# One weight load ahead of the attention loads, and weight splits held until the first block's last x

## The chip, the cores and the metric

The kernel runs on one core of a Trainium2 chip. The metric is the device time of one execution in microseconds (us); lower is better. TensorE (PE) has two clock levels, 1.2 and 2.4 GHz; the profile gives the granted clock as a share of the full one.

## The reference

The reference is a block-causal attention whose result goes through a mixture of four experts. Cut to what matters:

```python
# q, k, v: (4 batches, 8 heads, 576 positions, 64)
mask = pos_q // 64 >= pos_k // 64
attn = softmax(where(mask, q @ k.T / 8, -1e9)) @ v
x = attn.transpose(0, 2, 1, 3).reshape(2304, 512)
p = domain_probs / (domain_probs.sum(-1) + 1e-9)
for e in range(4):                       # w1[e]: 512 x 1024, w2[e]: 1024 x 512
    out += p[:, e:e+1] * (relu(x @ w1[e]) @ w2[e])
```

All data is fp32. The kernel gets enough precision out of fast matmuls by splitting every operand into a high half (a cast) and a low half (the operand minus the cast) and adding three products: high by high, low by high and high by low.

## The kernel before

**Tiles.** The 2304 tokens are cut into five blocks. Block 0 holds the first 64 positions of all four batches (256 tokens); blocks 1 to 4 hold the other 512 positions of one batch each. The attention of a block gives x, transposed, as `xh` (high) and `xl` (low). Block 0 needs only the first 64 keys, and a routine of its own, `first_block`, computes it in four steps (`step`, each one half of the batches and two of the four 128-row parts of x): transposes (L834), scores (L854), softmax on VectorE (DVE, L869 to L879) and ScalarE (ACT, L873), a transpose back (L883), the product with v (L896), and then the cast `xh` (L345) and the subtraction `xl` (L352). The steps run staggered; while PE has nothing to do in this prologue the program puts filler matmuls in (L364).

**Experts.** A chunk is one expert and 128 of its 1024 hidden columns: 32 chunks per block, numbered through. For each chunk `mm1` (L1013) forms h from x and w1 in 12 matmuls (four parts of x by three products), `relu` makes `hh` (ACT, L1030) and `hl` (DVE, L1032), and `mm2` (L1063) adds h by w2 to the accumulators (6 matmuls for block 0). Chunk i's mm2 is asked for after mm1 of chunk i + 1. Blocks 3 and 4 are done together, two chunks at a time, by seven products in place of eight (`product`, L1236), whose operands S1 to S4 are sums of x parts and whose weights `w1rp`, `w1l` and the like are sums of w1 quarters; `scp` are copies and sums of product results.

**Weights.** Each raw chunk of w1 and w2 is 256 KB. `w_load` brings it from memory into one of three buffers (`w1r`, `w2r`); `w_split` casts the high half (`w1h`, `w2h`, L345, ACT or DVE) and subtracts for the low half (`w1l`, `w2l`, L352, DVE). The raw buffer is free for the chunk three later as soon as both halves are there.

**Attention of the other blocks.** It goes on beside the expert matmuls, a pair of heads (a unit) at a time: K and Q are loaded (`kr`, `qr`), transposed on DVE (`kT` L415, `qT` L449), multiplied on PE (L509 and its kin, 2 groups of matmuls for the first units), and the scores are copied out by ACT (`S`, `cm`, masks L556).

**What sets the order.** No engine chooses at run time. A list scheduler, `Flow`, writes the whole program while the kernel is built: every operation has a cost, a priority (lower goes first) and inputs, the scheduler keeps a modelled clock for each engine, and it emits the operation that can start first, the lower priority number deciding among equals. Each engine then works through its own list in that order and stops at an instruction whose inputs are not there. All loads of raw weights, K, most of Q, and V stand in one list, that of SyncE (SP). While chunk 0 is at work (`now[0] == 0`), `w_prio` (L924) gives raw weights 1.6 (chunk 0) or 2.005 (all others); the next attention's K and Q have 2.00 and its V 2.005. A tuple `("until", condition)` holds a thread of the scheduler until the condition is true. `left_first[0]` counts the steps of `first_block` whose `xl` has not been emitted: 4 at the start, 0 after the last.

Of the kernel before, what the change touches and what calls it, by code (L numbers as in the profile page):

```python
# [210 lines left out]
def kernel(  # L211
# [131 lines left out]
    def a_copy(dst, src, n, r, u, prio=0.0, ps=False):  # L343
        engs = [("act", 0.833 * n + (55 if ps else 95)), ("dve", (1.04 if ps else 0.52) * n + 70)]
        o = op(engs, 0, lambda e: nc.scalar.copy(dst, src) if e == "act" else nc.vector.tensor_copy(dst, src), r, u, prio)  # L345
        o.port = not ps
        return o

    def tt(eng, dst, a, b, alu, n, r, u, prio=0.0):
        both = {"dve": 1.04 * n + 70, "pool": 2.1 * n + 365}  # L350
        engs = [(e, both[e]) for e in (eng if isinstance(eng, list) else [eng])]
        o = op(engs, 0, lambda e: ENG[e].tensor_tensor(out=dst, in0=a, in1=b, op=alu), r, u, prio)  # L352
        o.port = a.space != PSUM and b.space != PSUM
        return o
# [24 lines left out]
    now, loads = [0], [0]  # L379
    left_first = [len(STEPS)]  # L380
# [542 lines left out]

    def w_prio(i, which):  # L924
        i -= 4 * (i >= NC) * (which == 1)
        return lambda: (1.6 if i == 0 else 2.005) if now[0] == 0 else 1.0 if i <= now[0] + 1 else (2.5 if i <= now[0] + 2 else 5.0)

    def w_load(which, i, e, f):
        raw = yield fl.take(f"w{which}r")
        pr = w_prio(i, which)  # L930
        src = w1[e, :, f * P:(f + 1) * P].rearrange("(c p) f -> p c f", p=P) if which == 1 else w2[e, f * P:(f + 1) * P, :]
        v0 = yield dma(raw.tile, src, P * DM * 4, u=[raw], prio=pr)
        return raw, v0, pr

    def w_thread(which):
        for i, (_, e, f) in enumerate(chunks + [(PAIR, e, f) for e in range(E) for f in range(FC)]):
            if which == 1 and i >= NC:
                break
            raw, v0, pr = yield from w_load(which, i, e, f)
            fl.spawn(w_split(which, i, raw, v0, pr))  # L940
        if which == 1:
            for j, (e, f) in enumerate(pairs):
                got = []
                for k in range(2):
                    got.append((yield from w_load(1, NC + 2 * j + k, e, f + k)))
                fl.spawn(w_pair(j, *got))

    def flat(raw):
        return raw.tile.rearrange("p c f -> p (c f)") if len(raw.tile.shape) == 3 else raw.tile

    def halves(which, turn, src, n, deps, raw, pr, more=()):

        hi = yield fl.take(f"w{which}h", turn)
        lo = yield fl.take(f"w{which}l", turn)
        a = yield a_copy(hi.tile[:, :n], src, n, deps, [raw, hi], pr)
        o = tt(BOTH, lo.tile[:, :n], src, hi.tile[:, :n], SUB, n, deps + [a], [raw, hi, lo], pr)
        o.pen = lambda: 1000.0 if now[0] == 0 else 300.0
        l = yield o
        return hi, lo, a, l

    def w_split(which, i, raw, v0, pr):
        wt[i, which] = yield from halves(which, i, flat(raw), DM, [v0], raw, pr)
        fl.give(raw)

# [428 lines left out]
```

## Time and profile before

| what | us |
| --- | --- |
| median of 3 runs (lowest to highest) | 904.07 (903.63 to 905.41) |
| the profiled execution, its own time | 903.51 |
| span of the profiled execution, first to last instruction | 901.6 |
| PE busy in it | 890.2 |
| DVE busy in it | 692.3 |
| ACT busy in it | 451.8 |

The span is what the rows can explain; 1.9 us of the profiled execution lie around it. A row of a timeline gives start, duration, engine, line, operation, output and inputs, and in brackets the idle time of the engine before it and what ended that. The program's names come without buffer numbers there.

### The profile page before, as it was taken

What the parts mean: (1) busy time and instruction counts of PE and PEld (TensorE: products, weight loads), DVE (VectorE), ACT (ScalarE), POOL (GpSimd) and SP (SyncE); (2) the same over time, 40 slices, a digit from 0 to 9 for tenths busy, and PEclk for the clock granted to TensorE, in tenths of its full rate; (3) what the DMA queues carried; (4) which work ended last, traced back from release to release, by engine and by line L of the source; (5) the groups of instructions that cost most, each with busy time, mean ns of one, the idle gap of its engine ahead of it and who ended that gap; (6) DMA issues with size and microseconds to landing.
All of it is one profiled execution on the core that took longest, in us unless ns stands there. A gap on an engine that the chain in (4) does not pass through costs nothing.

```text
span 901.6 us, 12364 instructions
## 1 busy us (share of the span) xinstructions
PE 890.2 (99%) x4302; PEld 715.3 (79%) x4302; DVE 692.3 (77%) x1298; ACT 451.8 (50%) x857; POOL 140.6 (16%) x53
## 2 busy tenths in 40 slices
PE   8999999999999999999999999899999999999998
PEld 4778787787877877877877877688888888888886
DVE  6799999888988987988988888975566655566542
ACT  3587766564646556557645643545343333333220
POOL 1101110322133134124142232000000000000000
PEclk9999999999999999999999999999999999999999
DMA  9775457544535354634435332322120212110002
GB/s 179 171 199 168 146 142 185 157 109 96 144 95 126 103 128 104 172 118 114 103 109 118 93 95 75 123 72 59 35 68 27 82 35 71 48 48 24 12 1 94
DMA packets 214654, 91.17 MB, mean 101 GB/s; under 512 B 130368, under 2 KB 195904, under 8 KB 214592
## 3 DMA queue, kind: packets, MB, share of 16 engines
q1 hardware_dynamic: 211424, 89.59, 37.9%
q10 hardware_dynamic: 3168, 0.79, 0.5%
q8 instruction: 34, 0.56, 0.3%
q14 instruction: 28, 0.23, 0.1%
HBM read 85.63 MB, written 4.72 MB: 100 GB/s over the span
## 4 chain that ended last, share of the span: by engine, by line
PE 93%; DVE 3%; DMA 2%; SPq 1%; issue 0%; ACT 0%; DVEq 0%; ACTq 0%
PE h L1013 24%; PE acc L1063 23%; PE acc L1299 19%; PE h L1236 9%; PE att L1236 7%; PE att L733 4%; PE att L521 2%; PE att L522 2%; PE att L509 1%; PE acc L733 1%; DMA w1r<-in_moe_w_dram 1%; SPq L339 1%; DMA S<-in_v_dram 1%; PE acc L509 1%; DVE xr L352 1%; DMA cm<-in_q_dram 0%
## 5 line engine op out<-in xcount | busy, mean ns | idle before, releaser
L1013 PE MATMUL h<-xl,w1h 128*128 128x512 f32 (+1 forms) x384 | 136.5, 356 | 1.9 <-DVE xl L352 1.9
L1013 PE MATMUL h<-xh,w1h 128*128 128x512 f32 (+1 forms) x384 | 137.5, 358 | 0.0
L1013 PE MATMUL h<-xh,w1l 128*128 128x512 f32 (+1 forms) x384 | 136.5, 355 | 0.0
L1063 PE MATMUL acc<-w2h,hh 128*128 128x512 f32 x316 | 125.1, 396 | 0.0
L1063 PE MATMUL acc<-w2l,hh 128*128 128x512 f32 x316 | 123.4, 391 | 0.0
L1063 PE MATMUL acc<-w2h,hl 128*128 128x512 f32 x316 | 123.2, 390 | 0.0
L345 ACT CAST w2h<-w2r 128x512 fp32r<-128x512 f32 x113 | 70.4, 623 | 68.1 <-PE acc L1063 56.3
L666 POOL PARTITION_ALL_REDUCE sb<-sa x24 | 80.4, 3400 | 136.2 <-DVE sa L352 102.0
L687 POOL PARTITION_ALL_REDUCE mx<-cm x16 | 56.0, 3501 | 274.2 <-DVE cm L352 237.4
L352 DVE TENSOR_TENSOR w1l<-w1r,w1h 128x512 fp32r<-128x512 f32 (+1 forms) x124 | 86.5, 698 | 1.2 <-ACT w1h L345 0.3
L1030 ACT ACTIVATE hh<-h 128x512 fp32r<-128x512 f32 (+1 forms) x95 | 49.9, 526 | 72.0 <-PE h L1013 71.6
L352 DVE TENSOR_TENSOR w2l<-w2r,w2h 128x512 fp32r<-128x512 f32 x117 | 79.5, 680 | 4.7 <-ACT w2h L345 4.4
L1013 PEld LDWEIGHTS h<-xl,w1h 128*128 128x128 f32 x384 | 73.1, 190 | 12.4 <-DVE xl L352 2.1
L1013 PEld LDWEIGHTS h<-xh,w1h 128*128 128x128 f32 x384 | 72.9, 190 | 11.6 <-issue 1.2
L1013 PEld LDWEIGHTS h<-xh,w1l 128*128 128x128 f32 x384 | 73.0, 190 | 10.3
L345 ACT CAST w1h<-w1r 128x512 fp32r<-128x512 f32 (+1 forms) x111 | 66.1, 595 | 15.7 <-DMA w1r<-in_moe_w_dram 8.0
L1063 PEld LDWEIGHTS acc<-w2h,hl 128*128 128x128 f32 x316 | 59.3, 188 | 13.0
L1063 PEld LDWEIGHTS acc<-w2h,hh 128*128 128x128 f32 x316 | 59.5, 188 | 12.7 <-issue 1.7
L345 ACT COPY S<-att 128x512 f32<-128x512 f32 (+2 forms) x95 | 50.9, 536 | 34.6 <-DVE att L591 24.1
L1063 PEld LDWEIGHTS acc<-w2l,hh 128*128 128x128 f32 x316 | 59.5, 188 | 10.3
L1032 DVE SCALAR_TENSOR_TENSOR hl<-h,hh 128x512 fp32r<-128x512 f32 (+1 forms) x95 | 56.0, 589 | 9.9 <-ACT hh L1030 9.2
L352 DVE TENSOR_TENSOR S<-S,mx 128x1024 f32<-128x1024 f32 (+4 forms) x80 | 59.8, 790 | 3.3 <-POOL mx L687 3.1
(331 smaller groups left out, 1819.3 us busy)
## 6 DMA issues: line engine op xcount, KB each, us to landing
w2r<-in_moe_w_dram SPq DMA_DIRECT2D x128, 256.0 KB, 2.9
w1r<-in_moe_w_dram SPq DMA_DIRECT2D x120, 256.0 KB, 2.9
qr<-in_q_dram SPq DMA_DIRECT2D x112, 64.0 KB, 2.3
kr<-in_k_dram SPq DMA_DIRECT2D x64, 72.0 KB, 2.9
VN<-in_v_dram SPq DMA_DIRECT2D x32, 128.0 KB, 2.5
out_dram<-o SPq DMA_DIRECT2D x12, 256.0 KB, 2.1
w1rp<-in_moe_w_dram SPq DMA_DIRECT2D x8, 256.0 KB, 2.8
out_dram<-op SPq DMA_DIRECT2D x4, 256.0 KB, 2.1
```

The source lines that it names most:

```text
L345: o = op(engs, 0, lambda e: nc.scalar.copy(dst, src) if e == "act" else nc.vector.tensor_copy(dst, src), r, u, prio)
L352: o = op(engs, 0, lambda e: ENG[e].tensor_tensor(out=dst, in0=a, in1=b, op=alu), r, u, prio)
L509: nc.tensor.matmul(out=o, lhsT=KK.tile[hp, k0:k0 + n], rhs=qT.tile[hp, lo:W], start=True, stop=True)
L666: sums.append((yield op("pool", 150 + 6.3 * W, lambda _, h=h: nc.gpsimd.partition_all_reduce(sb.tile[:, h * W:h * W + W], sa.tile[:, h * W ...
L687: lambda _: nc.gpsimd.partition_all_reduce(mx.tile[:, :2 * W], src, P, RED.max),
L733: nc.tensor.matmul(out=x.tile[64 * g:64 * g + 64, W - w:W], lhsT=lhsT, rhs=rhs, start=(i == 0), stop=(i == len(todo) - 1))
L1013: nc.tensor.matmul(out=ps[:, :n], lhsT=s.tile[:, ks], rhs=x.tile[:, kc, :n], start=(kc == 0 and m == 0), stop=(kc == KC - 1 and m == 2),)
L1030: a = yield op("act", 0.833 * n + 55, lambda _: nc.scalar.activation(hh.tile[:, :n], ps[:, :n], AF.Relu), [mm], [pb, hh], 0.0)
L1032: l = yield op("dve", 1.04 * n + 70, lambda _: nc.vector.scalar_tensor_tensor(out=hl.tile[:, :n], in0=ps[:, :n], scalar=0.0, in1=hh.tile[: ...
L1063: nc.tensor.matmul(out=acc, lhsT=s.tile[:, ts], rhs=w.tile, start=(f == 0 and m == 0), stop=(f == FC - 1 and m == 2))
L1236: nc.tensor.matmul(out=ps[:, :n], lhsT=w.tile[:, ks], rhs=x[:, kc, :n], start=(start and kc == 0 and m == 0), stop=(i in (2, 3, 4) and kc ...
L1299: nc.tensor.matmul(out=acc, lhsT=s.tile[:, ts], rhs=w.tile, start=(c == 0 and x == 0), stop=(c == 3 and x == 2))
```

## The change

Two edits. In `w_prio`, while chunk 0 is at work, the raw w1 of chunk 1 (i = 1, which = 1) gets priority 1.7, which is ahead of K, Q and V of the next attention. In `w_split`, every split but those of w1 of chunks 0 and 1 waits until all four steps of the first block have their `xl` emitted.

```diff
     def w_prio(i, which):
         i -= 4 * (i >= NC) * (which == 1)
-        return lambda: (1.6 if i == 0 else 2.005) if now[0] == 0 else 1.0 if i <= now[0] + 1 else (2.5 if i <= now[0] + 2 else 5.0)
+        return lambda: (1.6 if i == 0 else 1.7 if i + which == 2 else 2.005) if now[0] == 0 else 1.0 if i <= now[0] + 1 else (2.5 if i <= now[0] + 2 else 5.0)
...
     def w_split(which, i, raw, v0, pr):
+        if i + which > 2 or (i, which) == (0, 2):
+            yield ("until", lambda: left_first[0] == 0)
         wt[i, which] = yield from halves(which, i, flat(raw), DM, [v0], raw, pr)
         fl.give(raw)
```

`i + which == 2` also holds for (0, 2), the w2 of chunk 0, but there the first condition, i == 0, has been taken. Lines behind L961 are two higher in the changed kernel.

Since the scheduler lists everything anew, the order changes on every engine from the prologue on. In DVE's list, at the end of the first block, the last two `xl` stood like this before (`xl_93` is x's low half; chunk n's halves have the numbers 61 + n, 65 + n, 69 + n and 73 + n for w1h, w1l, w2h and w2l):

```order
L352 TENSOR_TENSOR w1l_66<-w1r_78,w1h_62 128x512
L352 TENSOR_TENSOR xl_93<-acc_131,xh_91 128x2x128
L345 CAST w1h_63<-w1r_79 128x512
L352 TENSOR_TENSOR w1l_67<-w1r_79,w1h_63 128x512
L345 CAST w2h_70<-w2r_81 128x512
L352 TENSOR_TENSOR w2l_74<-w2r_81,w2h_70 128x512
L352 TENSOR_TENSOR xl_93<-acc_130,xh_91 128x2x128
L415 STREAM_TRANSPOSE kT_110<-kr_107 128x576
```

and stand like this now:

```order
L878 RECIPROCAL st_98<-st_98 128x4
L879 TENSOR_TENSOR o_90<-o_90,st_98 128x256
L352 TENSOR_TENSOR xl_93<-acc_131,xh_91 128x2x128
L352 TENSOR_TENSOR xl_93<-acc_133,xh_91 128x2x128
L415 STREAM_TRANSPOSE kT_110<-kr_107 128x576
L352 TENSOR_TENSOR w2l_73<-w2r_80,w2h_69 128x512
L352 TENSOR_TENSOR w1l_67<-w1r_79,w1h_63 128x512
L352 TENSOR_TENSOR w2l_74<-w2r_81,w2h_70 128x512
```

The last two `xl` follow one another; w1 of chunk 2 and w2 of chunk 1 (two casts and two subtractions), which stood between them, went to ACT (casts) and behind `xl` (subtractions), and so did w2l of chunk 0. The split of chunk 1's w1 (`w1h_62`, `w1l_66`), which stood ahead of the third `xl`, is now some rows earlier, among the softmax of the third step.

In ACT's list behind the last `xh`, before (`hh_83` is chunk 0's relu and `w2h_72` the cast of chunk 3's w2; `S`, `cm` belong to the first unit):

```order
L345 CAST w2h_71<-w2r_82 128x512
L1030 ACTIVATE hh_83<-h_128 128x256
L345 CAST w1h_64<-w1r_77 128x512
L345 CAST w2h_72<-w2r_80 128x512
L345 COPY S_120<-acc_132 128x512
L345 COPY cm_122<-acc_132 128x64
```

and now, some rows further on, where `hh_83` is chunk 2's relu and `w1h_62` the cast of chunk 5's w1:

```order
L345 COPY cm_122<-att_134 128x64
L556 ACTIVATE att_135<-ident 64x64 x2
L556 ACTIVATE acc_133<-ident 64x64 x2
L345 CAST w2h_72<-w2r_80 128x512
L345 COPY S_120<-att_135 128x512
L345 CAST w1h_62<-w1r_79 128x512
L556 ACTIVATE acc_132<-ident 64x2x64
L1032 ACTIVATE hh_83<-h_128 128x256
```

The cast of chunk 3's w2 left its place ahead of the scores' copies; it stands behind two of them, two `cm` copies and four masks now, four rows ahead of the relu of chunk 2.

In SP's list, where that w2 is loaded (`w2r_80`), before (`kr_108`, `VN_117` and `probs_n` are K, V and the domain probabilities for unit 1 and block 0):

```order
L339 DMA kr_108<-in_k_dram 32x18x32 x2
L339 DMA w2r_80<-in_moe_w_dram 128x512
L339 DMA kr_108<-in_k_dram 32x18x32
L339 DMA VN_117<-in_v_dram 128x64
L339 DMA VN_117<-in_v_dram 128x4x64
L339 DMA VN_117<-in_v_dram 128x64
L339 DMA VN_117<-in_v_dram 128x4x64
L339 DMA probs_n<-in_moe_domain_probs_dram 64x4 x4
```

and now (`w1r_78` is chunk 4's w1, `kr_107` is K of unit 2):

```order
L339 DMA kr_108<-in_k_dram 32x18x32 x3
L339 DMA VN_117<-in_v_dram 128x64
L339 DMA VN_117<-in_v_dram 128x4x64
L339 DMA w1r_78<-in_moe_w_dram 128x4x128
L339 DMA VN_117<-in_v_dram 128x64
L339 DMA VN_117<-in_v_dram 128x4x64
L339 DMA probs_n<-in_moe_domain_probs_dram 64x4 x4
L339 DMA kr_107<-in_k_dram 32x18x32 x4
L339 DMA w2r_80<-in_moe_w_dram 128x512
```

`w2r_80` moved behind V, the probabilities, chunk 4's w1 and the four loads of unit 2's K. Ahead of this place, chunk 1's `w1r_78` moved from behind unit 0's K, Q and V to ahead of them; the three raw loads that followed it (`w1r_79`, `w2r_81`, `w2r_82`) kept their places.

In DVE's list in the stage of the two blocks together (`scp` are sums of products, and `w1l_65` is the low half of the sum `w1rp` of w1 quarters), before:

```order
L352 TENSOR_TENSOR scp_4856<-h_128,scp_4859 128x512
L352 TENSOR_TENSOR w1l_68<-w1rp_4851,w1h_64 128x256
L352 TENSOR_TENSOR w2lp_4850<-w2r_82,w2hp_4848 128x512
L352 TENSOR_TENSOR w1rp_4851<-w1rp_4851,w1r_79 128x256
L1281 SCALAR_TENSOR_TENSOR hlp_4841<-scp_4856,hhp_4837 128x512
L352 TENSOR_TENSOR scp_4858<-scp_4857,scp_4858 128x512
L352 TENSOR_TENSOR w2l_74<-w2r_80,w2h_70 128x512
L352 TENSOR_TENSOR w1l_65<-w1rp_4851,w1h_61 128x512
```

and now, starting two rows behind the same first sum `scp`, which is `scp_4858` here:

```order
L352 TENSOR_TENSOR w2l_74<-w2r_80,w2h_70 128x512
L352 TENSOR_TENSOR w1rp_4853<-w1rp_4853 128x256
L352 TENSOR_TENSOR scp_4860<-scp_4859,scp_4860 128x512
L1283 SCALAR_TENSOR_TENSOR hlp_4843<-scp_4858,hhp_4839 128x512
L352 TENSOR_TENSOR w1l_68<-w1rp_4853,w1h_64 128x256
L352 TENSOR_TENSOR w2l_75<-w2r_81,w2h_71 128x512
L1283 SCALAR_TENSOR_TENSOR hl_86<-scp_4860,hh_84 128x512
L1283 SCALAR_TENSOR_TENSOR hlp_4844<-att_135,hhp_4840 128x512
L352 TENSOR_TENSOR w1rp_4853<-w1rp_4853,w1r_79 128x256
L352 TENSOR_TENSOR w2l_76<-w2r_82,w2h_72 128x512
L352 TENSOR_TENSOR xr_100<-att_134,xr_100 128x512
L352 TENSOR_TENSOR w1l_65<-w1rp_4853,w1h_61 128x512
```

`w1l_65` stands seven rows behind the first `scp` sum before, and thirteen behind it now. In PE's list the last 1525 instructions, from this stage on, are the same in both.

## Rows read from the trace of the kernel before

**Rows 1.** The page's first part: engine, busy time, share of the span, instructions.

```profile
PE 890.2 (99%) x4302; PEld 715.3 (79%) x4302; DVE 692.3 (77%) x1298; ACT 451.8 (50%) x857; POOL 140.6 (16%) x53
```

**Rows 2.** PE's waits: line, what was waited for, total, times, longest.

```profile
PE att L1236 <- ACT scp L1256: 2.0, 2, 1.4
PE h L1013 <- DVE xl L352: 1.9, 1, 1.9
```

**Rows 3.** PE's timeline, from block 0's first mm1 to unit 1's scores.

```profile
24.61 0.28 PE L1013 MATMUL h<-xh,w1h 128*128 128x256 f32 x1
26.76 0.58 PE L1013 MATMUL h<-xl,w1h 128*128 128x256 f32 x1 [1.86 <-DVE xl L352]
...
29.06 0.41 PE L1013 MATMUL h<-xh,w1l 128*128 128x256 f32 x1
29.40 1.03 PE L509 MATMUL acc<-qT,kT 64*128 64x512 f32 x1
...
31.71 0.39 PE L1013 MATMUL h<-xh,w1h 128*128 128x256 f32 x1
...
37.99 0.28 PE L1013 MATMUL h<-xh,w1h 128*128 128x256 f32 x1
...
39.42 0.40 PE L1063 MATMUL acc<-w2h,hh 128*128 128x512 f32 x1
...
43.03 0.69 PE L509 MATMUL att<-qT,kT 64*128 64x512 f32 x1
...
45.01 0.50 PE L1063 MATMUL acc<-w2h,hh 128*128 128x512 f32 x1
```

**Rows 4.** A stretch of core 0: us, busy time by engine, granted clock (PEclk), DMA.

```profile
26.70:30.10 3.40, 3.34 (x13) 2.93 (x15) 3.23 (x7) 1.41 (x3) 0.00 (x0) 0.50 0.72 169
```

**Rows 5.** DVE's timeline around the last `xl` of block 0.

```profile
24.15 0.43 DVE L345 CAST w1h<-w1r 128x512 fp32r<-128x512 f32 x1 [1.02 <-DMA w1r<-in_moe_w_dram]
...
25.68 0.69 DVE L352 TENSOR_TENSOR w2l<-w2r,w2h 128x512 fp32r<-128x512 f32 x1
26.29 0.42 DVE L352 TENSOR_TENSOR xl<-acc,xh 128x256 fp32r<-128x256 f32 x1
26.62 0.77 DVE L415 STREAM_TRANSPOSE kT<-kr 128x576 f32<-128x576 f32 x1
```

**Rows 6.** ACT's timeline: the last `xh`, a weight cast, a relu.

```profile
24.04 0.37 ACT L345 CAST xh<-acc 128x256 fp32r<-128x256 f32 x1 [1.20 <-PE acc L896]
...
37.09 0.61 ACT L345 CAST w2h<-w2r 128x512 fp32r<-128x512 f32 x1
...
39.63 0.38 ACT L1030 ACTIVATE hh<-h 128x256 fp32r<-128x256 f32 x1 [1.44 <-PE h L1013]
```

**Rows 7.** SP's issues; a row can hold several, as xN says.

```profile
24.32 1.02 SPq L339 DMA_DIRECT2D w2r<-in_moe_w_dram  x1
25.39 0.43 SPq L339 DMA_DIRECT2D kr<-in_k_dram  x1
...
28.14 2.43 SPq L339 DMA_DIRECT2D probs_n<-in_moe_domain_probs_dram  x4
30.67 1.08 SPq L339 DMA_DIRECT2D w1r<-in_moe_w_dram  x2
...
33.40 2.84 SPq L339 DMA_DIRECT2D qr<-in_q_dram  x4
```

**Rows 8.** Raw w2 loads issued up to 45 us, from issue to landing.

```profile
DMA to landing us min/median/max: 3.3/4.0/7.0
```

**Rows 9.** PE's timeline in the stage of two blocks together.

```profile
579.08 0.49 PE L1236 MATMUL att<-S4h,w1h 128*128 128x512 f32 x1 [1.37 <-ACT scp L1256]
...
583.76 0.39 PE L1236 MATMUL h<-S2h,w1l 128*128 128x512 f32 x1
```

**Rows 10.** DVE's timeline in the same stage.

```profile
577.21 0.68 DVE L352 TENSOR_TENSOR scp<-h,scp 128x512 f32<-128x512 f32 x1
...
580.88 0.68 DVE L352 TENSOR_TENSOR w1l<-w1rp,w1h 128x512 fp32r<-128x512 f32 x1
```

## The prediction

> **What bounds the kernel now.** I read the page's first part: PE is busy 890.2 of 901.6 us [rows 1], so only a wait or a slow clock on PE can give time back, and only a new PE wait can take it. PE's waits come second [rows 2]: two causes of some size are left, one `h<-xl` wait of 1.9 us in the first block and two `scp` waits of 2.0 us in all in the stage of two blocks together. The timeline of PE [rows 3] shows the first: the matmul at 26.76 had waited 1.86 us for block 0's last `xl`. DVE's timeline [rows 5] says why `xl` was late. ACT had the last `xh` at 24.04 + 0.37 = 24.41 [rows 6], but DVE was at four weight instructions, the first of which waited 1.02 us for its load (24.15), and `xl` ran from 26.29 to 26.71. The windows [rows 4] show the price behind the wait: the granted clock was 0.50 from 26.7 to 30.1, that is 1.2 GHz.
>
> **The last x.** Each term is made against the profiled execution, 903.51 us; the median is 904.07, so I add 0.56 at the end. In DVE's new order the last `xl` follows the third, with no weight work between. Chunk 1's cast and subtraction stand among the softmax now and w2l of chunk 0 has left it, so the softmax carries one cast more, 0.43 us [rows 5]; part of it falls into gaps between dependent steps, and I take 0.3 (bounds 0 to 0.43). `xh` then ends at 24.71, `xl` 0.42 later at 25.13, and with the 0.05 us between `xl` and matmul that 26.71 and 26.76 show, PE goes on at 25.18. That is 1.58 us earlier. PE has hardly a wait left there: its first seven matmuls end at 24.61 + 0.28, and 0.3 later than that.
>
> **The clock.** Without the pause I expect no slow stretch. From 26.76 to 29.40 stand eleven matmuls in 2.64 us [rows 3]; at the full clock twelve of the same kind take 39.42 - 37.99 = 1.43, so eleven take 1.31: 1.33 lost. The first group of scores took 31.71 - 29.40 = 2.31, its twin of unit 1 took 45.01 - 43.03 = 1.98: 0.33 lost. The two edits' gain is 1.58 + 1.33 + 0.33 = 3.24.
>
> **What the held splits cost at once.** The weight work that stood ahead of `xl` stands behind it. ACT does four casts behind the last `xh`, of 0.61 us at most [rows 6], 2.0 to 2.4 in all, then chunk 0's relu of 0.38: 27.1 to 27.5. PE has 5 + 12 matmuls to do meanwhile, 2.02 us, until 27.2. Its third matmul of mm2 needs `hl`, which on DVE stands behind `kT` (0.77 [rows 5]) and three subtractions (0.61 each by the starts 25.68 and 26.29): 25.13 + 0.7 + 1.83 + 0.42 = 28.1, against a need at some 27.7. That is 0.4. The scores need `qT`, one subtraction and one transpose behind `hl`, 29.3 against 29.0: 0.3. Together +0.7 (0 to 1.2, the upper end if both relu and `hl` are at their late ends).
>
> **Chunk 3's w2.** This is the term that I trust least. Before, its load was issued at 24.32 [rows 7]. Now fourteen issues come ahead of it from that place on: one K, four V, four probabilities, one w1, four K. Before, the nine issues from 25.39 to 30.67 took 0.59 each; the four Q from 33.40 on took 0.71 each, and a lone K 0.43. So the load is issued at 24.32 + 14 x 0.59 = 32.6 (30.3 to 34.3), and 4.0 us later (3.3 to 7.0 [rows 8]) it has landed: 36.6. ACT's list has the cast, a score copy, the next cast, masks and then chunk 2's relu, some 2.2 us as the sum of three times 0.61 and 0.38 [rows 6], so `hh` of chunk 2 is there at 38.8. What is queued behind the waiting cast is that relu, and PE waits for it with mm2 of chunk 2. PE was there at 39.42 [rows 3]; with 3.24 gained and 0.7 lost it is there at 36.9. New wait: 38.8 - 36.9 = 1.9. Ends: 30.3 + 3.3 + 2.2 = 35.8, no wait at all, and 34.3 + 7.0 + 2.2 = 43.5, 6.6 us.
>
> The row at 24.15 shows a cast that stood still for its load with `xl` behind it [rows 5]. The Trainium skill says the same for ACT (Perfetto Trace Analysis, Per-engine timelines): ACT, DVE and GpSimd are strict first-in first-out queues. It speaks against this change: by it the relu, whose h is long ready, cannot pass the cast. If it could, this term would be zero and the sum 1.9 lower.
>
> **Later loads.** Behind that w2 two more raw loads are issued, then eight loads of Q and probabilities and only then w1 of chunk 6: 32.6 + 3 x 0.59 + 2.84 + 2.43 = 39.6 [rows 7]. The weights of chunks 6 and 7 and w2 of chunk 5 thus come about 2 us later than before, but PE too is late by now, and they are wanted some chunks further on. I take +0.4 (0 to 2).
>
> **The stage of two blocks.** No operation is added there, yet DVE's list changed. `w1l_65` ended at 580.88 + 0.68 = 581.56 [rows 10], 2.2 us ahead of its use at 583.76 [rows 9]. Now twelve instructions stand between the sum `scp` and it: eight of 512 columns at 0.6 and four of 256 columns at 0.33 (the starts 26.29 and 26.62 in [rows 5]), so that with `scp` itself it starts 0.6 + 4.8 + 1.3 = 6.7 behind `scp`'s start (before: 580.88 - 577.21 = 3.7). Directly ahead of S4's low half three subtractions took the place of one cast and two small sums, 0.5 more. End: 577.21 + 0.5 + 6.7 + 0.68 = 585.1, which is 1.35 us late. The copies that the wait of 1.37 at 579.08 [rows 9] hangs on might come up to 0.3 us sooner, but `w1l_65` is last then, so that gains nothing. +1.35 (0, if DVE gets ahead earlier in the stage, to 1.9).
>
> **The sum.** -3.24 + 0.7 + 1.9 + 0.4 + 1.35 = +1.1: 904.6 for the profiled execution, 905.2 as a median.
>
> **Rivals.**
> First, the gain stays. If SP issues at the pace of the lone K (0.43), chunk 3's w2 is there in time and the loads behind it too: -3.24 + 0.7 + 1.35 = -1.2, a median of 902.9; if DVE also catches up in the late stage, -2.5, 901.5. [...] Against it: the nine issues at 0.59 were the same V and probabilities.
>
> Second, slower: the new wait costs the clock too. A pause of 1.86 us was followed by a stretch at 0.50 [rows 3, 4], while behind the pause of 1.37 matmuls took 0.39 [rows 9], as at full clock. A wait of 1.9 for chunk 3's w2 lies at the upper of these; from about there on, the 1.66 us of clock loss come back, and 905.2 becomes 906.9. With the slowest landing of [rows 8], 3 us above the 4.0, it would be 909 or more.
> [...]
>
> Third, the change does not do what it says. If chunk 1's w1 has not landed when its cast comes up among the softmax, DVE stops there, as it did for 1.02 us at 24.15, and the last `xl` is no earlier by that much: about +1 us, 906.2, or more if the clock falls as before.
>
> **How the numbers follow.** Forecast 905.2 with 0.45; the gain stays 0.27; the clock falls again or the load lands late 0.23; no earlier x 0.05. A run can tell about 0.2%, 1.8 us, from no change, so faster means below 902.3 and slower above 905.9. The first rival lies below 902.3 in about half of its cases, and 0.03 of the forecast with it: 0.17. The forecast's own spread (903.5 to 906.8, from the bounds of the small terms) puts 0.15 of it above 905.9; with 0.21 of the second rival and 0.05 of the third, slower has 0.41. Within 0.2% is left with 0.42: 0.27 of the forecast, 0.13 of the first rival, 0.02 of the second. The range reaches to both neighbours: 901.4, the first rival's lower time, to 908.3, between the two prices of the second.
>
> **What would show it.** In the changed kernel's profile: PE's wait `h<-xl` gone or under 0.4, no stretch at half clock from 25 to 30 us, the first mm2 at about 27.2 with a short wait for `hl`. SP issues `w2r` of chunk 3 past 32 us, and ACT stands before its cast with `<-DMA w2r`. PE waits for ACT's `hh` at about 37 us, 1 to 2 us long. Near 580 us PE waits for `w1l<-w1rp` or its cast. I am wrong if `w2r` is issued before 30.5 us, or if the late stage waits as before, or if a new wait shows between 45 and 560 us, where I put none.

## The result, and the profile after

| kernel | median, us | lowest to highest | ratio to before, 95% interval |
| --- | --- | --- | --- |
| before | 903.85 (6 runs) | 901.54 to 905.69 | |
| changed | 908.58 (6 runs) | 907.80 to 909.54 | 1.0058 [1.0040, 1.0076] |

The change costs 4.7 us. Slower was the forecast's sign, but the time lies 3.4 us above the 905.2 forecast and just outside the range. The profiled execution of the changed kernel took 908.19 us, its span is 906.4.

The page's first part of the changed kernel (engine, busy time, share, instructions) answers to [rows 1]; PE's work is the same, and its share fell:

```profile
PE 890.0 (98%) x4304; PEld 711.7 (79%) x4305; DVE 693.1 (76%) x1300; ACT 449.2 (50%) x855; POOL 142.8 (16%) x53
```

PE's waits in the changed kernel (line, what was waited for, total, times, longest) answer to [rows 2]; rows of the prologue are left out:

```profile
PE acc L1065 <- ACT hh L1032: 2.3, 2, 1.3
...
PE att L1238 <- ACT scp L1258: 1.4, 2, 0.7
PE att L733 <- DVE cm L352: 0.9, 2, 0.5
...
PE acc L509 <- ACT cm L345: 0.8, 1, 0.8
PE h L1238 <- ACT w1h L345: 0.7, 1, 0.7
...
PE h L1238 <- DVE w1l L352: 0.4, 1, 0.4
...
PE att L522 <- DVE LL L352: 0.3, 1, 0.3
PE att L570 <- DVE cm L352: 0.2, 1, 0.2
```

The wait for `xl` is gone. In its place stand two for a relu (`hh`), one for a copy of scores, four small ones for DVE in the middle of the kernel, and two for weights in the late stage. The slow stretch of [rows 4] is gone too. The same window in the changed kernel (us; busy time of PE, PEld, DVE, ACT, POOL; granted clock; DMA share; GB/s) reads:

```profile
26.70:30.10 3.40, 3.39 (x18) 1.95 (x19) 2.61 (x5) 1.73 (x5) 0.00 (x0) 1.00 0.41 90
```

PE's timeline answers to [rows 3]. The idle time in brackets understates a wait, since the matmul behind it also holds up its successor (the start after 36.54 comes 0.34 us later, where 0.23 is usual):

```profile
25.95 0.40 PE L1065 MATMUL acc<-w2h,hh 128*128 128x512 f32 x1
26.18 0.40 PE L1065 MATMUL acc<-w2l,hh 128*128 128x512 f32 x1
26.61 0.50 PE L1065 MATMUL acc<-w2h,hl 128*128 128x512 f32 x1
...
27.83 0.69 PE L509 MATMUL acc<-qT,kT 64*128 64x512 f32 x1
...
36.54 0.50 PE L1065 MATMUL acc<-w2h,hh 128*128 128x512 f32 x1 [0.99 <-ACT hh L1032]
...
43.87 0.50 PE L1065 MATMUL acc<-w2h,hh 128*128 128x512 f32 x1 [1.27 <-ACT hh L1032]
...
51.38 0.43 PE L509 MATMUL acc<-qT,kT 64*128 64x192 f32 x1 [0.76 <-ACT cm L345]
```

ACT's timeline in the same stretch shows what the two relus stood behind:

```profile
34.26 0.62 ACT L345 CAST w2h<-w2r 128x512 fp32r<-128x512 f32 x1 [2.96 <-DMA w2r<-in_moe_w_dram]
34.79 0.58 ACT L345 COPY S<-att 128x512 f32<-128x512 f32 x1
35.26 0.62 ACT L345 CAST w1h<-w1r 128x512 fp32r<-128x512 f32 x1
...
36.12 0.36 ACT L1032 ACTIVATE hh<-h 128x256 fp32r<-128x256 f32 x1
...
41.42 0.62 ACT L345 CAST w1h<-w1r 128x512 fp32r<-128x512 f32 x1 [3.35 <-DMA w1r<-in_moe_w_dram]
41.95 0.58 ACT L345 COPY S<-acc 128x512 f32<-128x512 f32 x1
42.43 0.62 ACT L345 CAST w1h<-w1r 128x512 fp32r<-128x512 f32 x1
42.95 0.59 ACT L345 COPY S<-att 128x512 f32<-128x512 f32 x1
43.42 0.40 ACT L1032 ACTIVATE hh<-h 128x256 fp32r<-128x256 f32 x1
```

And SP's issues, the changed kernel's answer to [rows 7]:

```profile
26.47 2.43 SPq L339 DMA_DIRECT2D probs_n<-in_moe_domain_probs_dram  x4
29.00 2.15 SPq L339 DMA_DIRECT2D kr<-in_k_dram  x4
31.25 0.44 SPq L339 DMA_DIRECT2D w2r<-in_moe_w_dram  x1
31.79 0.39 SPq L339 DMA_DIRECT2D w1r<-in_moe_w_dram  x1
32.26 0.45 SPq L339 DMA_DIRECT2D w2r<-in_moe_w_dram  x1
32.81 1.98 SPq L339 DMA_DIRECT2D qr<-in_q_dram  x4
34.83 2.52 SPq L339 DMA_DIRECT2D probs_n<-in_moe_domain_probs_dram  x4
37.46 0.93 SPq L339 DMA_DIRECT2D w1r<-in_moe_w_dram  x2
```

**Where the time went.** But for fillers, both kernels do the same matmuls. I lined up equal PE instructions of the two traces and took start in the changed kernel minus start in before. A step in this difference is time lost or gained there:

| us in before | 21 | 27 | 36 | 42 | 52 | 95 | 232 | 254 | 291 | 365 | 431 | 562 | 584 | last matmul |
| --- | --- | --- | --- | --- | --- | --- | --- | --- | --- | --- | --- | --- | --- | --- |
| changed, us | -1.12 | -3.11 | -4.11 | -2.66 | +0.35 | +0.06 | +0.08 | +1.31 | +1.91 | +1.91 | +2.71 | +2.68 | +3.68 | +3.69 |

The first -1.12 is no effect of the change: the profiled execution of before began its first block late (the first `xs` matmul at 16.20 us; most other executions here have it between 14.5 and 15.1), because PE was slow for longer at its start. The three filler matmuls before its second transposes and the same three in the changed kernel:

```profile
6.77 1.49 PE L364 MATMUL h<-const-bfloat16-1.0 128*128 128x512 bf16 x3
```

```profile
6.49 0.81 PE L364 MATMUL h<-const-bfloat16-1.0 128*128 128x512 bf16 x3
```

Measured from 21 us on, the change gains 2.99 us by 36, gives back 1.45 by 42 and 3.01 by 52, loses 2.60 between 232 and 562 and 1.00 in the late stage. The end adds 1.1 for the last output writes (a median of 3.2 us from issue to landing, 2.1 before), which the late start of before happens to cancel.

### The profile page after: what moved, and what is told of

The parts are those of the page before. It is cut to its first block, busy times and chain, and to the rows that moved or that the text cites. A ratio compares the mean times of both kernels' runs of the same rounds, so it can differ in the third digit from the quotient of the medians.

```text
span 906.4 us, 12380 instructions
## 1 busy us (share of the span) xinstructions
PE 890.0 (98%) x4304; PEld 711.7 (79%) x4305; DVE 693.1 (76%) x1300; ACT 449.2 (50%) x855; POOL 142.8 (16%) x53
## 4 chain that ended last, share of the span: by engine, by line
PE 83%; DVE 11%; DMA 2%; ACT 1%; issue 1%; SPq 1%; POOL 0%; DVEq 0%; ACTq 0%; POOLq 0%
PE acc L1301 19%; PE h L1015 19%; PE acc L1065 19%; PE h L1238 9%; PE att L1238 6%; PE att L733 4%; PE att L521 2%; PE att L522 2%; DVE S L352 1%; DVE w1l L352 1%; DVE w2l L352 1%; DVE o L1102 1%; DVE hl L1034 1%; SPq L339 1%; PE acc L733 1%
```

## The experiments

Two kinds of kernels. The first three are the changed kernel's code with one edit, or part of one, undone. The others take the choice away from the scheduler: each engine gets its rows in the order of a table, which is the recorded order of before or of the changed kernel, or a mix, or one with rows moved by hand. Their lines stand 30 below those of before. The core of that edit is:

```diff
-            first = min(cands, key=lambda c: (c[0][0], c[1][1].prio()))
...
+            rank, eng, (who, nth, n) = min((q[0][0], e, q[0][1]) for e, q in self.todo.items() if q and q[0][1][:2] in at)
+            self.todo[eng].pop(0)
+            th = at[who, nth]
...
+TABLE = "..."
```

A ratio is to the runs of before that were timed beside the kernel.

### Which edit, and which part of the program

The load alone (`w_split` as before):

```diff
-        if i + which > 2 or (i, which) == (0, 2):
-            yield ("until", lambda: left_first[0] == 0)
```

> Only the priority of chunk 1's raw w1 is changed; no split is held. Theory A (the first stage's gain is the early last x, its loss is late weights whose casts stand ahead of a relu on ScalarE): weight work stays ahead of the last x, so PE's wait for xl stays at 1 to 2 us with a stretch at half clock behind it, and chunk 3's w2 is issued near 24 us as before, so there is no wait for a relu near 37 us. In the first 60 us within 1 us of before. Theory B (the early load itself is the harm, because K, Q and V come later): PE waits for scores of the first units, 2 us or more slower in the first 60 us. Either way the order behind is drawn anew, which may add 0 to 4 us.

Measured: 905.98 us, 1.0030 [1.0020, 1.0041]. The `xl` wait was gone, which my theory denied: the other loads' order alone had redrawn DVE's list, so this run does not separate early load and held splits. PE gains 3.1 us from 21 to 36 us; at 232 us the difference is still -0.83, at 431 us +1.32, at 584 us +2.30. So the middle and the late stage lose their 2.1 and 1.0 us without any held split.

The hold alone (`w_prio` as before):

```diff
-        return lambda: (1.6 if i == 0 else 1.7 if i + which == 2 else 2.005) if now[0] == 0 else 1.0 if i <= now[0] + 1 else (2.5 if i <= now[0] + 2 else 5.0)
+        return lambda: (1.6 if i == 0 else 2.005) if now[0] == 0 else 1.0 if i <= now[0] + 1 else (2.5 if i <= now[0] + 2 else 5.0)
```

> Only the splits are held; chunk 1's raw w1 keeps its old priority. Theory A: the last x is early (no wait for xl over 0.5 us, no half-clock stretch from 25 to 30 us), chunk 3's w2 is issued past 30 us, and PE waits for relus of chunks 2 and 4, 2 us together; in all 2 to 5 us slower than before, like the full change. Theory B (the load is what matters): as fast as before within 1.8 us.

Measured: 905.45 us, 1.0022 [1.0012, 1.0033]. `xl` still makes PE wait twice, 0.8 in all; the gain goes to two copies of scores, and behind them the granted clock was 0.50 from 35.8 to 39.2 us. PE's waits in it:

```profile
PE acc L509 <- ACT cm L345: 1.9, 1, 1.9
...
PE att L509 <- ACT cm L345: 1.0, 1, 1.0
```

Chunk 0's w2 not held, so that chunk 3's w2 is loaded early as before:

```diff
-        if i + which > 2 or (i, which) == (0, 2):
+        if i + which > 2:
```

> The full change, but chunk 0's w2 is not held, so its raw buffer is free early and chunk 3's w2 can be issued before V. Theory A: w2 of chunk 3 is issued near 25 us, no wait for the relu of chunk 2 near 37 us; the early x stays. First 60 us 1 to 3 us faster than before. The later order is drawn anew and may add up to 4 us, so in all -2 to +3 us against before. Rival C (the waits come from the early x alone: PE runs ahead of every load and waits for the next one anyway): waits of the same sum, 2 to 3 us, appear at other chunks.

Measured: 907.50 us, 1.0041 [1.0027, 1.0054]. An `hh` wait of 1.5 us shows at another place, and from 95 us on the differences are those of the changed kernel to 0.05 us (+1.30 at 254, +2.70 at 431, +3.67 at 584). Loading chunk 3's w2 early does not take the loss away.

The changed kernel's order up to the first mm1 of chunk 24 (122 us) and before's from there on:

> No scheduler choice: every engine follows a fixed list, that of the changed kernel until mm1 of chunk 24 (about 122 us) and that of the kernel before for all the rest. Theory A, by the two profiles: the first part costs 1.2 us, the middle and the late stage cost nothing: +1.2 us against before (0 to 2.2). Rival D (all of the loss sits in the first part and the later differences only shift it): +4 to +5 us.

Measured: 904.88 us, 1.0012 [1.0000, 1.0023]. From 122 us to the end the difference to before stays at +2.12 us, with no wait in the middle; so what is lost is lost in the first stage: 1.5 us by the medians. (The profiled execution lost 3.6 from its start of -1.48, with a score-copy wait of 1.93 us where the changed kernel has 0.76, and a stretch at half clock behind it that the changed kernel does not have:

```profile
52.10:55.50 3.40, 3.40 (x11) 2.25 (x10) 3.40 (x7) 3.40 (x8) 0.00 (x0) 0.50 0.76 256
```

So its 3.6 is no measure of the order alone.) The other way round, before's order up to chunk 24:

> A fixed list: the kernel before until mm1 of chunk 24 (about 122 us), the changed kernel's list for all the rest. Theory A, from the profile of the changed kernel: 2.6 us are lost between 190 and 430 us in waits for VectorE work of the attention that its list has later than PE's need (LL, cm), and 1.0 us near 580 us at w1h and w1l. So +3.6 us against before (2.5 to 4.5), with a slow first block left in place. Rival D (all the loss sits in the first part): within 1 us of before.

Measured: 906.89 us, 1.0043 [1.0028, 1.0059], repeated as mid_base below with 1.0046 [1.0031, 1.0060]. The difference goes from -1.51 at 122 us to +2.16: 3.67 us lost behind 122 us. The changed kernel's order only from chunk 88 (523 us) on:

> A fixed list: the kernel before until mm1 of chunk 88 (about 523 us), the changed kernel's list for the rest, the stage of two blocks above all. Theory A: only the waits for w1h and w1l near 583 us come with it, +1.0 us (0.6 to 1.4). Rival: they come only when DVE arrives late from the middle of the changed list; then 0.

Measured: 905.09 us, 1.0021 [1.0011, 1.0032], twice the expected loss. Of its 2.1 us, 1.2 arise between 505 and 548 us, at the seam (a wait of 0.8 for `cm`), where the changed kernel itself loses 0.1; joining two orders made a wait of its own. The step from 562 to 584 us is +1.00, with the two waits for `w1h` and `w1l`, as in the changed kernel.

So 1.2 (table above) to 1.5 us (after_then_before) of the loss belong to the first stage, 2.6 to the middle and 1.0 to the late stage.

### The first stage: moving single rows

The changed kernel's order from a table, as the base:

> The changed kernel's own order, written from a fixed list; the same instructions on every engine. Both theories: as the changed kernel, 4 to 5.5 us slower than before. It is the base of the three kernels below.

Measured: 907.75 us, 1.0062 [1.0045, 1.0079]: the table behaves as the code does. Then chunk 4's relu ahead of the split of chunk 6's w1, here on ACT:

```diff
 L1060 ACTIVATE hh_84<-h_129 128x256
+L1060 ACTIVATE hh_83<-h_128 128x256
 L375 CAST w1h_63<-w1r_77 128x512
...
-L1060 ACTIVATE hh_83<-h_128 128x256
```

> The changed kernel's list with one move: both halves of chunk 4's relu stand ahead of the splits of w1 of chunk 6, ScalarE's cast and VectorE's subtraction. Theory A (PE's wait of 1.27 us near 43.9 us is the cast of chunk 6's w1, which waits for its load, with the relu queued behind): this wait goes, 1.0 to 1.3 us faster than the changed kernel's list. Rival E (PE then waits for the score copies and w1 of chunk 6 instead): gain under 0.4 us.

Measured: 908.04 us, 1.0062 [1.0046, 1.0077]. The wait moved and did not shrink; PE's waits have no `hh` any more, but the one below, with the granted clock at 0.50 from 54.4 to 57.8 us behind it:

```profile
PE acc L539 <- ACT cm L375: 2.3, 1, 2.3
```

Chunk 3's w2 ahead of four K loads on SP:

```diff
-L369 DMA kr_107<-in_k_dram 32x18x32 x4
-L369 DMA w2r_80<-in_moe_w_dram 128x512
+L369 DMA w2r_80<-in_moe_w_dram 128x512
+L369 DMA kr_107<-in_k_dram 32x18x32 x4
```

> The changed kernel's list with one move: the raw load of chunk 3's w2 stands ahead of the four K loads of unit 2. Theory A: it is issued near 29 us and lands near 32.5, ScalarE's wait of 2.96 us at 34.26 shrinks to under 1 us and PE's wait of 0.99 us for the relu of chunk 2 goes. But the loads of chunk 6's w1 come no sooner, so the wait for the relu of chunk 4 grows by about as much: 0 to 0.4 us gained in all. Rival F (the two waits are independent): 1 us gained.

Measured: 908.89 us, 1.0070 [1.0051, 1.0089], no gain. The first `hh` wait is gone; one of 1.4 us is left at 44 us, behind a cast of w1 that stood 2.94 us for its load. (In the profiled execution the stretch from 21 to 95 us is 0.65 us shorter than in before, but that execution began 1.9 us later than after_list's, with the slow fillers of before; whether a late start and a short first stage go together is open, so I go by the medians.) Both moves together:

> The changed kernel's list with both moves. Theory A: both waits for relus go, 2.0 to 2.3 us faster than the changed kernel's list. Rival E: under 1 us, the waits move to the next weights.

Measured: 908.16 us, 1.0063 [1.0047, 1.0079]. My theory wanted 2 us. An `hh` wait of 1.5 is back, at 37 us, now behind a cast of w1 that stood 2.30 us for its load, and 0.6 for `probs_n` is new. Three kernels gained nothing, though two of them were rid of the wait they aimed at: another load was waited for in its place. That points to the queue that issues them.

Next the intended gain by itself, without the change: before's order, and on DVE alone the last `xl`, `kT` and `qT` ahead of two weight splits.

```diff
-L345 CAST w1h_63<-w1r_79 128x512
-L352 TENSOR_TENSOR w1l_67<-w1r_79,w1h_63 128x512
-L345 CAST w2h_70<-w2r_81 128x512
-L352 TENSOR_TENSOR w2l_74<-w2r_81,w2h_70 128x512
 L352 TENSOR_TENSOR xl_93<-acc_130,xh_91 128x2x128
 L415 STREAM_TRANSPOSE kT_110<-kr_107 128x576
 L449 STREAM_TRANSPOSE qT_111<-qr_109 128x512
+L345 CAST w1h_63<-w1r_79 128x512
...
```

> The kernel before, fixed list, with one change on VectorE: the last xl, kT and qT stand ahead of the two splits (w1 of chunk 2, w2 of chunk 1) that stood before them; chunk 0's hl between those two splits. Nothing else moves, the whole later order is that of before. Theory A: PE's wait of 1.86 us and the stretch at half clock go, 3.2 to 3.5 us gained at 36 us; the weights of chunks 4 to 7 land no sooner, so 1 to 2 us of it are given back at 40 to 48 us in waits for relus and score copies. In all 1.5 to 2.5 us faster than before. Rival G (all is given back, since loads set the pace of the first chunks): within 0.5 us.

Measured: 903.42 us, 0.9999 [0.9988, 1.0010], where 1.5 to 2.5 us less was expected. Wait and slow stretch are gone, and PE gains 2.6 us between 21 and 42 us. By 52 us all of it is given back, in PE's timeline here:

```profile
44.38 0.59 PE L539 MATMUL att<-qT,kT 64*128 64x192 f32 x2 [1.09 <-ACT cm L375]
...
45.99 0.43 PE L539 MATMUL acc<-qT,kT 64*128 64x192 f32 x1 [1.03 <-ACT cm L375]
```

With the rows between these put in a better order too (chunk 4's relu forward on ACT and DVE, two weight casts on ACT behind the score copies):

> The list of x_last_first with three more moves: chunk 4's relu ahead of the split of w1 of chunk 6 on both engines, and the casts of w2 of chunk 6 and w1 of chunk 7 behind unit 1's score copies. Theory A: no cast that waits for its load stands ahead of a relu or a score copy that PE needs, so most of the gain stays: 2.5 to 3.4 us faster than before. Rival G: within 0.5 us of x_last_first, since mm1 of chunks 6 and 7 then waits for the loads themselves.

Measured: 902.20 us, 0.9986 [0.9975, 0.9997], a gain at the edge of what can be measured, where 2.5 to 3.4 us were expected. The runs lie within 1.5 us (901.44 to 902.98), where before's beside them lie between 900.3 and 906.5. The two large waits are down to one of 0.7, but the profile does not explain the gain: from 21 to 36 us PE wins 2.6 us, and by 72 us it has lost 3.3. The granted clock, on record for every timed run, bears on it: 11 of the 12 runs have 0.999 or more, with a median of 902.2 us, and of x_last_first's 12 runs 5, with a median of 902.3. So what the tuned order has over x_last_first shows as fewer runs with a slow clock.

### What sets the pace of the first stage

In SP's rows above, four loads of probabilities (64 x 4 numbers each; the later four 128 x 4) hold the queue for 2.43 us, as long as five weight loads of 256 KB. Eight such loads stand ahead of weights in the first 40 us and are not needed so early. I moved them behind w1 of chunks 9 and 11, and the DVE rows that read them behind accordingly. On SP:

```diff
 L369 DMA VN_117<-in_v_dram 128x4x64
-L369 DMA probs_n<-in_moe_domain_probs_dram 64x4 x4
 L369 DMA w1r_78<-in_moe_w_dram 128x4x128
...
 L369 DMA w2r_82<-in_moe_w_dram 128x512
-L369 DMA probs_n<-in_moe_domain_probs_dram 128x4 x4
 L369 DMA w2r_80<-in_moe_w_dram 128x512
```

Four kernels, each with this move: x_last_first's order,

> The list of x_last_first, with the eight small loads of the domain probabilities of blocks 0 and 1 (four of 64 rows, four of 128 rows) moved on SP from ahead of w1 of chunk 4 and w2 of chunk 6 to behind w1 of chunk 9 and of chunk 11, and their four DVE instructions each moved behind accordingly. Theory H (SP's list sets the pace of the first chunks: every issue takes about 0.55 us whatever its size, so eight small loads ahead of the weights cost some 4 us of SP time): weights of chunks 4 to 7 land 2 to 4 us sooner, the waits for score copies and relus between 42 and 52 us, 2.8 us in x_last_first, shrink under 1 us; 1.5 to 2.5 us faster than x_last_first and than before. Rival K (the DMA engines or ACT's own work set the pace): within 0.5 us of x_last_first.

before's order,

> The control: the kernel before with the same eight small loads moved, the last xl left late. There PE waits for nothing between 27 and 143 us, so theory H and rival K both say: within 0.5 us of before.

early_x_tuned's,

> early_x_tuned with the eight small loads moved. Theory H: the gain at 36 us is kept whole, 2.5 to 3.2 us faster than before. Rival K: as early_x_tuned, about 1.2 us faster than before.

and after_then_before's:

> after_then_before (the changed kernel's list until mm1 of chunk 24, the list of before for the rest) with the eight small loads moved. Theory H: w2 of chunk 3 is issued near 29 us in place of 31.2, w1 of chunk 6 near 33 in place of 37.5, and the waits for the relus of chunks 2 and 4 go, 2.2 us; 1.5 to 2.5 us faster than after_then_before, so about 1 us faster than before. Rival K: as after_then_before, about 1.1 us slower than before.

| order | without the move | with the move | median with it, us |
| --- | --- | --- | --- |
| x_last_first | 0.9999 [0.9988, 1.0010] | 0.9971 [0.9958, 0.9984] | 900.71 |
| before | 1 | 0.9981 [0.9969, 0.9993] | 901.37 |
| early_x_tuned | 0.9986 [0.9975, 0.9997] | 0.9983 [0.9972, 0.9994] | 901.73 |
| changed, then before's | 1.0012 [1.0000, 1.0023] | 0.9970 [0.9959, 0.9982] | 900.93 |

In the last of these the changed kernel's own first stage turns from a loss into a gain. SP's rows there:

```profile
26.66 2.07 SPq L369 DMA_DIRECT2D kr<-in_k_dram  x4
28.83 0.44 SPq L369 DMA_DIRECT2D w2r<-in_moe_w_dram  x1
...
32.60 1.57 SPq L369 DMA_DIRECT2D w1r<-in_moe_w_dram  x2
```

Chunk 3's w2 is issued 2.4 us sooner than in the changed kernel, chunk 6's w1 4.9 us sooner. ACT's casts of the two stood 2.97 and 3.05 us for their loads in after_then_before, and 0.89 and 0.55 here. Both `hh` waits are gone, and from 22 to 60 us PE's timeline has one wait left:

```profile
47.87 0.43 PE L539 MATMUL acc<-qT,kT 64*128 64x192 f32 x1 [0.63 <-ACT cm L375]
```

PE gains 3.0 us from 21 to 36 us and still has 1.4 of them at 122 us.

One of the four expectations came true, that of x_last_probs_late. after_probs_late gained 2.1 us on before where about 1 was expected, and the tuned order gained nothing over early_x_tuned. The control, before's order, was to stay within 0.5 us and gained 1.7. That expectation rested on the one profile of before, where PE waits for nothing between 27 and 143 us. Three other profiles have before's order up to 122 us (before_then_after, mid_base and mid_moved), and each waits 1.0 us for `cm` near 46 us, in before_then_after so:

```profile
45.50 0.43 PE L539 MATMUL acc<-qT,kT 64*128 64x192 f32 x1 [1.01 <-ACT cm L375]
```

In mid_base and mid_moved the granted clock behind it was 0.50 for 3.4 us. With the loads moved this wait is gone. (The control's `xl` waits 0.8 where before's waits 1.9, but that is not shown to come from the move: the order up to there is the same, and mid_moved, in before's order there, has 0.8 too.) Of the control's 12 runs 10 have a granted clock of 0.999 or more, with a median of 901.3 us; of before's 35 beside them 6, with a median of 902.3. So about 1 us of the 1.7 stands at a like clock, and the rest goes with the clock.

So the SP move has a value of its own, which does not simply add to that of the early `xl`; how the two share their gain I cannot say from these runs. Nor is it SP alone: the move takes eight rows off DVE's list in this stretch too, one of which stood 1.23 us for its load in x_last_first (30.07), and no kernel here moves the loads without these rows. The two fastest, 900.71 and 900.93 us, beat both kernels of this case.

### The middle

Behind 122 us nothing of the change is near; only the order differs. In attention unit 7, DVE does `LL` late. PE's and DVE's timelines of the changed kernel:

```profile
243.12 0.50 PE L522 MATMUL att<-LL,KK 128*128 128x512 f32 x1 [0.26 <-DVE LL L352]
...
248.57 2.81 PE L733 MATMUL att<-S,VN 128*64 128x512 f32 x20 [0.35 <-DVE cm L352]
```

```profile
241.85 1.22 DVE L352 TENSOR_TENSOR LL<-qT,HH 128x1024 fp32r<-128x1024 f32 x1
```

The row of before, where `LL` was done 4 us ahead of its use at 241.32 us:

```profile
234.80 2.31 DVE L352 TENSOR_TENSOR LL<-qT,HH 128x1024 fp32r<-128x1024 f32 x1
```

Is it the place of these rows, or is DVE late as a whole? In before_then_after's order I moved two rows on DVE:

```diff
+L382 TENSOR_TENSOR LL_115<-qT_111,HH_114 128x1024
 L382 TENSOR_TENSOR w1l_68<-w1r_79,w1h_64 128x512
 L382 TENSOR_TENSOR w2l_76<-w2r_82,w2h_72 128x512
...
-L382 TENSOR_TENSOR LL_115<-qT_111,HH_114 128x1024
...
+L382 TENSOR_TENSOR cm_122<-att_135,S_121 128x448
 L382 TENSOR_TENSOR w1l_66<-w1r_78,w1h_62 128x512
 L382 TENSOR_TENSOR sa_124<-sa_124,S_120 128x2x192
-L382 TENSOR_TENSOR cm_122<-att_135,S_121 128x448
```

> The list of before_then_after (before's order up to the first mm1 of chunk 24, the changed kernel's from there on) with two subtractions of DVE drawn forward in attention unit 7: `LL<-qT,HH` ahead of two splits of weights and four score subtractions, and `cm<-att,S` of 448 columns ahead of one weight split. In before_then_after PE is 1.20 us further behind the kernel before at 254 us than at 232 us, with waits of 0.3 for `LL` and 0.3 to 0.4 for `cm` there. If the place of these two rows on DVE makes the loss (theory M), both waits go, the step from 232 to 254 us falls from +1.20 to at most +0.4, and the run is 0.6 to 1.2 us faster than before_then_after of the same call. If DVE as a whole is too late in that stretch (rival: the weights that are pushed back are then waited for), the step stays at +0.8 or more, with a wait for `w1l` or `w2l` in place of the two, and the time is the same within 0.5 us.

> before_then_after once more, beside mid_moved on the same chip: both theories expect what it showed before, some 3.9 us over the kernel before (1.0043), a step of +1.2 us from 232 to 254 us, and waits for `LL` and `cm` of 0.3 us each there.

Measured: 908.08 us, 1.0055 [1.0035, 1.0075], against mid_base's 907.09 us, 1.0046 [1.0031, 1.0060]. The wait for `LL` went, but the step from 232 to 254 us grew from 1.24 to 2.34 us, in PE's timeline of mid_moved:

```profile
248.05 0.42 PE L551 MATMUL att<-HH,KK 128*128 128x320 f32 x1 [0.92 <-DVE cm L375]
...
254.08 0.47 PE L551 MATMUL att<-HH,KK 128*128 128x512 f32 x1 [1.06 <-DVE cm L382]
```

The score work pushed back behind `LL` is what PE waits for now. So drawing these two rows forward does not take the loss away. Whether DVE as a whole has too much due in this stretch, or another order of the same rows would do, was not tried; what in the redrawn order costs the 2.6 us stays open.

## Why the prediction was right and wrong

| term | forecast, us | measured, us |
| --- | --- | --- |
| early `xl`, clock, held splits (to 36 us) | -3.24 + 0.7 = -2.5 | -2.99 |
| chunk 3's w2 (36 to 42) | +1.9 | +1.45 |
| later loads (42 to 95) | +0.4 (0 to 2) | +3.01 - 0.29 = +2.7 |
| middle (95 to 562) | 0 | +2.6 |
| late stage (562 on) | +1.35 | +1.0 |
| sum | +1.1 | +4.8 |

**The gain: right.** No `xl` wait, no slow stretch. With the 1.12 us of before's later start added, the first mm2 stands at 27.07 (forecast 27.2) and the first scores at 28.95 (29.3). Before `hl`, two starts lie 0.43 apart where 0.23 is usual: 0.2 lost, 0.4 forecast.

**Chunk 3's w2: mechanism right, size a little too large.** The load was issued at 31.25, or 32.4 with the later start (forecast 32.6). It landed 2.99 us later, not 4.0 (less than the least of [rows 8], 3.3), so ACT had the relu at 36.48 and PE stood for 0.99 us. The Trainium skill's rule that ACT is strictly first-in first-out (Perfetto Trace Analysis, Per-engine timelines) agrees with the trace: the relu's matmuls were over at 35.55, but it ran at 36.12, behind a cast that had stood 2.96 us for its load.

**Later loads: the step that failed first.** I had w1 of chunk 6 issued at 39.6 (measured 37.46, or 38.6 with the later start), so its lateness was in the working. What failed is the sentence that these weights "are wanted some chunks further on". The matmuls want them later; ACT's list does not. The cast of chunk 6's w1 stands ahead of chunk 4's relu, stood 3.35 us for its load, and the relu behind it cost PE 1.27 us idle; a copy of scores at 51.38 cost 0.76 more. I had worked out exactly this mechanism for chunk 3's w2 and did not ask it of the next load. Taking away that wait alone gave nothing (relu4_first); taking eight small issues out of the way did (after_probs_late). So the term hung on how soon the weights are issued, not on one cast's place.

**The middle: the step that failed second.** I put no new wait between 45 and 560 us, and named one there as what would prove me wrong. I had looked at the order's differences where the change acts and in the late stage, and taken equal work to mean equal time elsewhere. before_then_after shows 3.67 us lost behind 122 us, 2.7 of them before 562, without any of the change's first stage. Why the redrawn order is slower there stays open; that it is, is shown.

**The late stage: right.** `w1h` and `w1l` are late near 584 us, by 0.69 and 0.42 us idle; the two `scp` waits fell from 2.0 to 1.4 in return.

**The rivals.** That the gain stays needed SP at the pace of a lone K; x_last_probs_late and after_probs_late show that it does stay where SP's queue is relieved. That the new wait costs the clock did not happen in the profile of the changed kernel: behind the waits of 0.99 and 1.27 us the granted clock stayed 1.00 (36 to 46 us). It did happen behind the longer waits of hold_only, relu4_first and after_then_before. That the measured time lies near its upper time of 909 is luck, by other means. The change did what it says. The lower end of the range, 901.4, is 901.5 by its own sum; nothing hangs on it.

## What to carry to other kernels

Where a scheduler draws the order, price a local edit over the whole program: replay the recorded order up to a point and switch, and the loss is placed in two runs. A weight load is due when its cast comes up in the list of an in-order engine, not when the matmul wants it; ask that of every load that moves. On a busy issuing queue count issues, not bytes: eight tiny loads ahead of the weights were worth more here than the edit itself. And before a gain is put down to a wait, compare the granted clock of all timed runs.

## What the runs showed of the hardware that was not expected

**The clock behind the same wait differs from run to run.** late_after and before_then_after have before's order up to 122 us. Both show the `xl` wait of 1.5 us. Windows from 24.00 to 31.50 us of before, late_after and before_then_after, in that order (columns as above):

```profile
24.00:31.50 7.50, 5.63 (x29) 4.24 (x29) 6.05 (x11) 3.00 (x8) 0.00 (x0) 0.77 0.52 111
```

```profile
24.00:31.50 7.50, 6.20 (x23) 4.14 (x23) 5.45 (x13) 3.11 (x7) 0.00 (x0) 0.54 0.58 134
```

```profile
24.00:31.50 7.50, 6.71 (x43) 4.83 (x43) 5.75 (x14) 4.88 (x14) 0.00 (x0) 1.00 0.69 172
```

The granted clock is 0.77, 0.54 and 1.00: of the 7.5 us about 3.5 at half clock ((1 - 0.77) / 0.5 x 7.5), about 6.9, or none. My clock term of 1.66 us is thus one draw. In the other profiles, behind the longest waits, 1.9 us in hold_only and after_then_before and 2.3 in relu4_first, the clock fell to 0.50 as in before; behind waits of 1.3 to 1.5 us in load_only, after_list, hold_later, both_moves and w2_3_sooner it stayed 1.00; and in mid_base it fell right behind a wait of 1.03 (46.37). Part of the spread of times comes from this: of the 121 runs of before timed beside the experiments, the 31 with a granted clock of 0.999 or more have a median of 902.3 us, the 61 with 0.997 or less 903.3. Runs of like clock still lie over 4 us apart.

**The clock at the start differs too.** In before the fillers at 6.77 start 0.43 us apart, in the changed kernel those at 6.49 start 0.22 apart, so before's ran at the lower of the two levels (the clock column of the windows has 1.00 there and does not show it). Six of the 20 profiled executions were slow like this between 6 and 10 us: before, before_probs_late, relu4_first, w2_3_sooner, x_last_probs_late and, from 7.6 us on, mid_moved. These six have the first `xs` matmul at 16.2 to 16.9 us, the other 14 at 14.5 to 15.1. The Trainium skill says that the number of slow matmuls at a kernel's start is run-variable (TensorE: Matmul & The Clock Gate, What's actually happening); these fillers agree.

**An issue costs SP about the same whatever it moves.** SP's issues in before, with shortest, median and longest in ns, for loads of probabilities (1 to 2 KB) and of raw w2 (256 KB):

```profile
L339 SPq DMA_DIRECT2D probs_n<-in_moe_domain_probs_dram x20: 424/430/596, 28.1 to 368.1; - x20
L339 SPq DMA_DIRECT2D w2r<-in_moe_w_dram x128: 327/340/1023, 7.7 to 834.1; - x128
```

Single issues are held far longer (a K load 3.35 us at 20.87 in before); what holds them was not read.
